# Output products of a threshold-attention and SwiGLU kernel: one level of seven-product blocks against two

## The chip, the cores and the metric

The kernel runs on one NeuronCore of a Trainium2 chip. Its five engines are TensorE (PE in the profile: matrix products into PSUM; PEld is its weight load), VectorE (DVE), ScalarE (ACT), GpSimd (POOL) and SyncE (SP, which here issues most of the DMAs). The metric is device time in microseconds, the median of several runs.

## The reference, cut to what matters

```
# q, k, v: (8, 8, 576, 64); w_gate, w_val: (512, 1536); w_out: (1536, 512), all float32
scores = matmul(q, k.T) / sqrt(64)
scores = where(scores >= max(scores) - tau, scores, -1e9)
attn   = exp(scores - max(scores));  attn = attn / (sum(attn) + 1e-9)
x      = matmul(attn, v)             # heads joined: x is (4608, 512)
g      = x @ w_gate
out    = (g * sigmoid(g) * (x @ w_val)) @ w_out
```

## The kernel before, in words

**Chunks.** The 4608 tokens are worked in nine chunks of 512. Chunks 0 to 7 hold the first 512 tokens of each of the eight batch entries, chunk 8 the 64 remaining tokens of all of them. For each chunk there are three kinds of TensorE work: attention (scores, L1173, and attention times values, L1260), gate and value products (`Group`, products issued at L890) and output products (`Outputs`, L1054).

**Seven products for eight.** Gate and value work is done in the Strassen-Winograd manner: a 2x2 block product takes seven block products and some sums of blocks. For the output product the two token halves of a unit of 256 tokens, the two halves of the 1536 inner columns and the two halves of the 512 output columns are the 2x2 blocks. So each of a chunk's two units has seven products (`one` to `seven`), each six matmuls with 128 tokens held and 256 output columns moved. Sums of the gated values (`half_sums`, 128x256 each) are made on POOL (L768), or on DVE (L771) in the tail. The results are added up in SBUF by DVE (L1073), POOL and ACT, and stored.

**Gated values.** `Group.finish` makes them: tanh on ACT (L943), a product on DVE (L944), a product on POOL (DVE in the tail). A group is 256 of the 1536 columns; a chunk has six groups of seven products (`p1` to `p7`), four matmuls each. Four of the seven weight operands of a group stay in SBUF (`wgv`, with one difference written over a quarter of it); the other three are sums that were computed once, stored in HBM (`sums_hbm`) and are loaded for each group into one of the two halves of `ring`.

**Slots.** From chunk 0 on the work is interleaved. A slot (`kk`, 0 to 19 for each batch entry `b`) is one tile of queries of a pair of heads: 128 queries, or 64 in the last of each five. In a slot TensorE first does the scores (`slot_scores`, two PSUM tiles; they must have been read by the slot before), in every fifth slot (`kk` 1, 6, 11, 16) the attention product of the five slots before, and then a written-out number of products as filler: `GV[kk]` steps of gate and value products of chunk `b-1`, then `CH[kk]` output products. Meanwhile DVE finds the maxima (L1195), ACT takes exponentials (L1209), DVE masks and sums (L1210), ACT and POOL scale (L1240, L1237), DVE transposes (L1241). After the last slot of `b` = 7 comes the tail, without softmax: the last attention, then chunks 7 and 8 with gate, value and output products only. There POOL's sums go to DVE.

**Order.** A planner (`Plan`) orders the small work while the program is built: each `job` has an engine, an assumed duration, dependencies and a rank (0 first); `pe` places TensorE work in program order. On the chip each engine runs its list in order and waits on semaphores.

**Early part.** Chunk 0's attention is done before the slots, with some 128x128 products (L450, L452, which turn the attention weights) that occur nowhere else.

Of the kernel before, what the change touches and what calls it, by code (L numbers as in the profile page):

```python
# [108 lines left out]
def kernel(  # L109
# [11 lines left out]
    nc = tc.nc  # L121
# [52 lines left out]
    wgv = const.tile([P, 2, NCC, DFF], F32, name="wgv")  # L174
    wo = const.tile([P, 2, NF, DM2], F32, name="wo")
    extra = const.tile([P, 3 * WS], F32, name="extra")
    ring = const.tile([P, 2, 3 * HW], F32, name="ring")
# [4 lines left out]
    ob = const.tile([P, 2, DM], F32, name="ob")  # L182
    sums_hbm = hbm.tile([NF2, P, 3 * HW], F32, name="sums_hbm")
    last_hbm = hbm.tile([P, NCC, B * (S - SM)], F32, name="last_hbm")

    rall = ring.rearrange("p s n -> p (s n)")
# [46 lines left out]
    los = deque([extra[:, 4 * S + 2 * TW:], rall[:, 4 * S:], ob.rearrange("p i n -> p (i n)")[:, 0:TW]])  # L233
# [529 lines left out]

    def ring_part(s, n):
        return ring[:, s, n * HW:(n + 1) * HW].rearrange("p (k f) -> p k f", k=2)

# [47 lines left out]
    def weight_sums(g, place, *deps):  # L814
# [5 lines left out]
        stores[g] = job("SP", 0.1, lambda: nc.sync.dma_start(out=sums_hbm[g], in_=place), j, lag=4.0)  # L820
# [6 lines left out]
    loads = {}  # L827

    def load_sums(c, g, *deps):
        loads[c, g] = job("SP", 0.1, lambda: nc.sync.dma_start(out=ring[:, g % 2], in_=sums_hbm[g]), stores[g], *deps, lag=4.0)  # L830
# [47 lines left out]
    class Group:  # L878


        def __init__(self, c, g):
            self.c, self.g = c, g
            self.b = None

# [9 lines left out]
        def ring_w(self, n):  # L894
            return ring_part(self.g % 2, n)

# [5 lines left out]
        def p1(self, early=True):  # L902
            self.a = take("pa")
            self.m1 = self.mul(self.a, pair_cols(wval, 0, self.g), x_block(self.c, 0, 0), True, *self.a.deps, *ready_x[self.c][0])
            self.a.bank.full = True
            if early:
                self.take_b()

        def p5(self):
            self.take_b()  # L910
            self.e = take("pe")
            m = self.mul(self.e, self.ring_w(0), xs[0], True, loads[self.c, self.g], *ready_x[self.c][1], *self.e.deps)
# [5 lines left out]
        def p2(self):  # L918
# [5 lines left out]
            m = self.mul(self.a, pair_cols(wval, 1, self.g), x_block(self.c, 0, 1), False, self.cb if self.b else self.s1)  # L924
            self.m2 = m

        def p6(self):
            u = self.u1_buf
            if self.b:
                m = self.mul(self.b, self.ring_w(1), xs[1], False, self.cb, *ready_x[self.c][2])  # L930
            else:
                b = self.b = take("pb")
                m = self.mul(b, self.ring_w(1), xs[1], True, *ready_x[self.c][2], *b.deps)
# [3 lines left out]
            self.u1 = job("ACT", 0.55, lambda: nc.scalar.activation(u.ap, self.b.rows(), AF.Copy, scale=0.5), m, *self.u1_old, rank=0)  # L937

# [550 lines left out]
```

## Time and profile before

| | us |
|---|---|
| median of three runs | 1440.7 (1439.89 to 1440.7) |
| profiled execution, its own time | 1440.44 |
| its span | 1438.7 |
| early part, to the first interleaved slot | 0 to 143 |
| interleaved slots (`b` = 1 to 7) | 143 to 1200 |
| period of an interleaved chunk | 154.5 |
| chunk 7 in the tail | 1215.8 to 1325.3 |
| chunk 8 in the tail | 1325.3 to 1438.7 |
| last output product ends | 1434.2 |

The DMA engines moved 77 GB/s in the mean and up to 203 GB/s in one fortieth of the span (slice 2). In the lines of the profile, "xN" is a number of records and "mean" is for one record; the columns after the bar are the busy time in us, the mean duration in ns, and the time that the engine sat idle just before such instructions, with what ended it. An answer on stretches lists, for each, its length and for each engine the busy time in us and the number of instructions, then the clock granted to TensorE, the DMA share and GB/s. A timeline line has the start, the length from first start to last end, the engine, line, operation and the number of records; the durations of neighbouring matmul records overlap, so their spacing is read from the starts. A wait line has the total, the number of times and the longest.

### The profile page before, as it was taken

The page shows a single profiled execution, that of the slowest core. Times are in us where ns is not written, and L with a number is a line of the kernel's source. Part 1 is how long each engine was busy: PE and PEld are TensorE (multiplying, and loading weights), DVE is VectorE, ACT ScalarE, POOL GpSimd, SP SyncE. Part 2 cuts the span into 40 slices and gives each one's busy share as a digit, 9 for nine tenths or more (in the row PEclk, how much of TensorE's full clock was granted, in tenths as well). Part 3 has the DMA queues.
Part 4 walks back from the last instruction along what each step waited for, and adds up shares of the span by engine and source line. Part 5 has one row for each costly group of instructions (what it writes and reads, how often), then busy time and mean ns, then how long its engine had stood idle before and what let it go on. Part 6 is the DMA issues. An engine that isn't in the chain of part 4 may idle for free.

```text
span 1438.7 us, 31145 instructions
## 1 busy us (share of the span) xinstructions
PE 1400.7 (97%) x11496; PEld 1078.7 (75%) x11496; DVE 1061.6 (74%) x3045; ACT 794.0 (55%) x2170; POOL 697.8 (49%) x686
## 2 busy tenths in 40 slices
PE   9999899999999999999999999999999999999998
PEld 6676666777777777777777777777777777888887
DVE  7988999888777878788788877887788874343343
ACT  6888765566646665566546664566556652220220
POOL 2465759965574448444754466445745462000000
PEclk9999999999999999999999999999999999999999
DMA  8734312353223312333232222332223311112101
GB/s 177 203 120 133 66 34 79 115 139 78 56 71 87 79 49 63 82 78 78 56 81 54 72 78 50 95 78 54 63 69 78 78 39 56 66 45 80 64 25 30
DMA packets 192071, 111.47 MB, mean 77 GB/s; under 512 B 165040, under 2 KB 166064, under 8 KB 191920
## 3 DMA queue, kind: packets, MB, share of 16 engines
q1 hardware_dynamic: 188320, 109.05, 28.5%
q8 instruction: 92, 1.51, 0.5%
q10 hardware_dynamic: 3600, 0.43, 0.2%
q14 instruction: 59, 0.48, 0.1%
HBM read 94.24 MB, written 15.20 MB: 76 GB/s over the span
## 4 chain that ended last, share of the span: by engine, by line
PE 76%; DVE 13%; ACT 6%; issue 2%; SPq 2%; DMA 1%; DVEq 0%; ACTq 0%
PE po L1054 22%; PE pb L890 14%; PE pa L890 10%; PE pe L890 10%; PE xa L1260 8%; PE sc L1173 7%; DVE pall L1210 3%; DVE mx L1195 2%; ACT pall L1209 2%; DVE pall L1241 1%; DVE mx L1201 1%; SPq L317 1%; DVE hall L944 1%; PE pv L498 1%; ACT sums L1224 1%
## 5 line engine op out<-in xcount | busy, mean ns | idle before, releaser
L1237 POOL TENSOR_SCALAR pall<-pall,ri 128x288 f32<-128x288 f32 x224 | 223.7, 1012 | 154.5 <-DVE ri L1230 153.4
L1210 DVE SCALAR_TENSOR_TENSOR pall<-sc,th,pall 128x288 f32<-128x288 f32 x504 | 233.1, 510 | 64.4 <-ACT pall L1209 63.3
L1209 ACT ACTIVATE pall<-sc,nm 128x288 f32<-128x288 f32 x504 | 213.6, 495 | 9.0 <-DVE pall L1210 9.0
L1195 DVE TENSOR_REDUCE mx<-sc 128x2 f32<-128x576 f32 x252 | 179.3, 747 | 38.2 <-PE sc L1173 37.2
L1054 PE MATMUL po<-wo,hall 128*128 128x256 f32 x852 | 196.2, 382 | 1.3 <-DVE hall L944 0.9
L1054 PEld LDWEIGHTS po<-wo,hall 128*128 128x128 f32 x852 | 159.6, 190 | 34.5 <-issue 5.8
L890 PE MATMUL pb<-xall,ring 128*128 128x256 f32 x768 | 184.5, 383 | 0.0
L890 PE MATMUL pa<-xall,wgv 128*128 128x256 f32 x768 | 183.3, 381 | 0.0
L1241 DVE STREAM_TRANSPOSE pall<-pall 128x1152 f32<-128x1152 f32 (+1 forms) x140 | 174.9, 1251 | 6.0 <-ACT pall L1240 3.5
L1205 ACT ACTIVATE th<-nm,cut 128x4 f32<-128x4 f32 (+1 forms) x140 | 41.5, 297 | 243.7 <-DVE nm L1202 219.6
L890 PEld LDWEIGHTS pb<-xall,ring 128*128 128x128 f32 x768 | 143.4, 190 | 31.9 <-issue 10.8
L1173 PE MATMUL sc<-kT,qT 64*32 64x288 f32 x4032 | 156.6, 410 | 9.1 <-DVE pall L1210 7.6
L890 PEld LDWEIGHTS pa<-xall,wgv 128*128 128x128 f32 x768 | 144.1, 190 | 27.6 <-ACT tmp L916 2.8
L768 POOL TENSOR_TENSOR hall<-hall,tmp 128x512 f32<-128x512 f32 x79 | 100.5, 1275 | 104.8 <-DVE hall L944 58.1
L1224 ACT COPY sums<-sums 32x4 f32<-32x4 f32 (+1 forms) x560 | 108.4, 194 | 74.7 <-DVE pall L1210 66.0
L1240 ACT ACTIVATE pall<-pall,ri 128x288 f32<-128x288 f32 x280 | 133.9, 529 | 26.6 <-DVE ri L1230 25.2
L1260 PE MATMUL xa<-pall,vall 64*64 64x288 f32 x2016 | 135.7, 409 | 12.3 <-DVE pall L1241 8.7
L1260 PEld LDWEIGHTS xa<-pall,vall 64*64 64x64 f32 x2016 | 88.4, 134 | 58.7 <-DVE pall L1241 12.0
L1173 PEld LDWEIGHTS sc<-kT,qT 64*32 64x32 f32 x4032 | 59.0, 105 | 79.2 <-issue 49.1
L1054 PE MATMUL po<-extra,ring 128*128 128x256 f32 x432 | 97.8, 382 | 0.6 <-DVE ob L1073 0.6
L1054 PEld LDWEIGHTS po<-extra,ring 128*128 128x128 f32 x432 | 80.9, 190 | 17.5 <-POOL hall L768 3.3
L890 PE MATMUL pe<-xall,ring 128*128 128x256 f32 x384 | 92.0, 382 | 0.0
(171 smaller groups left out, 2152.1 us busy)
## 6 DMA issues: line engine op xcount, KB each, us to landing
ring<-sums_hbm SPq DMA_DIRECT2D x48, 768.0 KB, 4.5
vall<-in_v_dram SPq DMA_DIRECT2D x112, 144.0 KB, 2.9
out_dram<-ob SPq DMA_DIRECT2D x32, 256.0 KB, 2.1
qT<-in_q_dram SPq DMA_DIRECT2D x112, 72.0 KB, 3.4
kT<-in_k_dram SPq DMA_DIRECT2D x112, 72.0 KB, 2.8
wo<-in_moe_w_gate_dram SPq DMA_DIRECT2D x16, 384.0 KB, 3.6
wo<-in_moe_w_val_dram SPq DMA_DIRECT2D x16, 384.0 KB, 4.1
sums_hbm<-ring SPq DMA_DIRECT2D x4, 768.0 KB, 4.2
```

Of the source, the lines that this page charges most:

```text
L768: return lambda: nc.gpsimd.tensor_tensor(out=out, in0=a, in1=b, op=op)
L890: nc.tensor.matmul(ps[:, i], w[:, k_, i * P:(i + 1) * P], x[:, k_, :], start=first and i == k_ == 0, stop=True, skip_group_check=True)
L1054: nc.tensor.matmul(ps, h(f), w[:, f, :], start=(f == 0), stop=(f == NF2 - 1))
L1173: nc.tensor.matmul(ps[g * G:(g + 1) * G, h, 0:SH], qT[hs, col:col + G], kT[hs, c * SH:(c + 1) * SH], start=True, stop=True)
L1195: rs.append(job("DVE", 0.72, lambda x=x, tile_=tile_: nc.vector.tensor_reduce(out=mx[:, 2 * x:2 * x + 2, 0], in_=tile_[:, :, 0:SH], axis=A ...
L1209: ej = job("ACT", 0.42, lambda x=x: nc.scalar.activation(ps[x], scs[x], AF.Exp, bias=nm[:, x:x + 1]), ej, rank=0)
L1210: mj = job("DVE", 0.45, lambda x=x: nc.vector.scalar_tensor_tensor(out=ps[x], in0=scs[x], scalar=th[:, x:x + 1], in1=ps[x], op0=ALU.is_ge, ...
L1224: nc.scalar.copy(sm[g * G:(g + 1) * G, 0:m, 1], sm[o * G:(o + 1) * G, 0:m, 0])
L1237: scaled.append(job("POOL", 1.02, lambda x=x: nc.gpsimd.tensor_scalar(out=ps[x], in0=ps[x], scalar1=ri[:, x:x + 1], scalar2=None, op0=ALU. ...
L1240: scaled.append(job("ACT", 0.46, lambda x=x: nc.scalar.activation(ps[x], ps[x], AF.Copy, scale=ri[:, x:x + 1]), rj, rank=2))
L1241: seg["turned"].append(job("DVE", 0.72 * len(pss), lambda: nc.vector.transpose(out=whole, in_=whole), *scaled, rank=2 if t < NT else 1))
L1260: nc.tensor.matmul(holds[a].ap()[h * D:(h + 1) * D, 0:SH].rearrange("d (i q) -> d i q", q=G), vr[rs, h, j, :], p[rs, h, :, j, :], start=(j ...
```

## The change

For chunks 2 to 8 the output product of a whole chunk (512 tokens) is done by a class `Deep` instead of `Outputs`. Its outer 2x2 blocks are 256 tokens, 768 inner columns and 256 output columns; each of the seven outer products is itself split into seven products of blocks of 128 tokens, 384 inner columns and 128 output columns (`product`, 49 in all, three matmuls each with 128 moved columns). An outer product's seven inner results stand side by side in two PSUM banks (896 columns). The outer additions are made by letting a product accumulate onto the banks of an earlier one after ACT has copied the earlier state to SBUF (`copies`), or by DVE adds; the inner ones are made once per output block in `combine`, four small additions. The sums of gated values are made in two layers: 128x512 outer sums (`sum`) and four 128x384 sums for each outer operand (`inner_sums`), shared between DVE and POOL.

The seven outer weight operands are split further once, by `deepen` (28 sums on POOL, in slots 2 to 8 of `b` = 3); the results lie where `wgv` was. So from chunk 2 on all seven weight operands of a gate and value group are loaded from HBM for each group, in two parts (`load_flow`), into `flow`, which covers the old `ring` and part of `wgv`; `store_plain` writes the four plain ones there once. `Deep` also uses `flow` for its sums and asks for the next chunk's loads when it is done with them.

The slots are laid out anew: other numbers in `GV` (for chunk 1 too), `CD` for the deep output steps, and in the nine slots of `BY_ACT` ACT does all four scalings instead of POOL two. In the tail `Deep` has an order of its own.

```diff
+    whole = const.tile([P, OB + 2 * NCC * DFF + 2 * 3 * HW], F32, name="big")
+    obs, big = whole[:, 0:OB], whole[:, OB:]
+    wgv = big[:, 0:2 * NCC * DFF].rearrange("p (m c f) -> p m c f", m=2, c=NCC)
-    ring = const.tile([P, 2, 3 * HW], F32, name="ring")
+    ring = big[:, 2 * NCC * DFF:].rearrange("p (s n) -> p s n", s=2)
+    flow = big[:, 2 * NCC * DFF + 2 * 3 * HW - 2 * GW:]
+    deeper = big[:, 0:NQ * 3 * QW]
...
+    def store_plain(g, *deps):
+
+        js = []
+        for n, w in ((0, pair_cols(wval, 0, g)), (1, pair_cols(wval, 1, g)), (5, pair_cols(wgat, 1, g)), (6, pair_cols(wgat, 0, g))):
+            js.append(job("SP", 0.1, lambda n=n, w=w: nc.sync.dma_start(
+                out=sums_hbm[g][:, n * HW:(n + 1) * HW].rearrange("p (k f) -> p k f", k=2), in_=w), *deps, lag=4.0))
+        plain_stores[g] = js
...
+    def load_flow(c, g, part, *deps):
+        lo, to = ((0, 4), (4, NQ))[part]
+        s = g % 2 * GW
+        loads[c, g, part] = job("SP", 0.1, lambda: nc.sync.dma_start(
+            out=flow[:, s + lo * HW:s + to * HW], in_=sums_hbm[g][:, lo * HW:to * HW]), stores[g], *plain_stores[g], *deps, lag=6.0)
...
+            ways = (lambda: pair_cols(wval, 0, g), lambda: pair_cols(wval, 1, g), lambda: ring_part(g % 2, 0), lambda: ring_part(g % 2, 1),
+                    lambda: ring_part(g % 2, 2), lambda: pair_cols(wgat, 1, g), lambda: pair_cols(wgat, 0, g))
+            self.w = [way() if c < DEEP else flow_part(g % 2, n) for n, way in enumerate(ways)]
+            self.w_deps = [[loads[c, g] if n in (2, 3, 4) else parts[g] if n == 6 else None] if c < DEEP else
+                           [loads[c, g, n // 4]] for n in range(NQ)]
...
+            if self.c >= DEEP and self.g + 2 < NF2:
+                load_flow(self.c, self.g + 2, 0, plan.t + plan.PIPE)
...
             if self.g + 2 < NF2:
-                load_sums(self.c, self.g + 2, m)
+                if self.c < DEEP:
+                    load_sums(self.c, self.g + 2, m)
+                else:
+                    load_flow(self.c, self.g + 2, 1, m)
...
+    operands = w11, w21, w22, ws4, w12, ws2, ws3
...
+    def quarters(a):
+
+        h = NF2 // 2
+        return [a[:, y * h:(y + 1) * h, x * P:(x + 1) * P] for y in range(2) for x in range(2)]
+
+    def deepen(o, *deps):
+        b11, b12, b21, b22 = quarters(operands[o])
+        t1, t2, t4 = (deeper_part(o, n) for n in range(3))
+        j = job("POOL", 1.0, pool_tt(t1, b12, b11, ALU.subtract), *deps, rank=3)
+        j = job("POOL", 1.0, pool_tt(t2, b22, t1, ALU.subtract), j, rank=3)
+        j = job("POOL", 1.0, pool_tt(t4, b21, t2, ALU.subtract), j, rank=3)
+        deep_jobs[o] = [job("POOL", 1.0, pool_tt(b12, b22, b12, ALU.subtract), j, rank=3)]
...
+            KW = NF2 * TC
+            self.s2, self.s3 = (flow[:, lo:lo + KW].rearrange("p (f n) -> p f n", n=TC) for lo in (GW, GW - KW))
+            self.early_place, self.late_place = flow[:, 0:KW], flow[:, 2 * GW - KW:2 * GW]
...
+            if tail[0]:
+                self.steps = deque([self.p1, self.gates_end, self.p2, self.p7_alone, self.p5, self.p6_alone, self.p3, self.p4_alone])
+                self.spaces = [pall[:, n * CW:(n + 1) * CW] for n in range(5)]
+            else:
+                self.steps = deque([self.p1, self.gates_end, self.p2, self.p5, self.p6, self.p3, self.p7, self.p4])
+                self.spaces = [*spaces, None, spaces[1]]
+            self.ready["a11"] = [gated[c, 0, x] for x in range(NF2 // 2)]
+            self.inner_sums(0, self.a11, self.early_place, self.ready["a11"], mark)
...
+        def early(self, mark):
+            c, n = self.c, NF2 // 2
+            j3 = [self.sum(self.s3, self.a11, self.a21, ALU.subtract, x, self.ready["a11"][x], gated[c, 1, x], mark) for x in range(n)]
+            self.ready["s3"] = j3
+            self.ready["s1"] = [self.sum(self.a21, self.a21, self.a22, ALU.add, x, j3[x], gated[c, 1, n + x]) for x in range(n - 1)]
+            if tail[0]:
+                self.inner_sums(6, self.s3, pall[:, 5 * CW:5 * CW + NF2 * TC], j3)
+
+        def late(self, mark):
+            c, n = self.c, NF2 // 2
+            self.ready["a12"] = [gated[c, 0, n + x] for x in range(n)]
+            self.ready["a22"] = [gated[c, 1, n + x] for x in range(n)]
+            j3 = self.ready["s3"]
+            self.inner_sums(1, self.a12, self.a11, self.ready["a12"], self.m1, *j3)
+            self.ready["s1"].append(self.sum(self.a21, self.a21, self.a22, ALU.add, n - 1, j3[n - 1], gated[c, 1, NF2 - 1], dve=True))
+            self.inner_sums(4, self.a21, self.late_place, self.ready["s1"], mark)
+            self.ready["s2"] = [self.sum(self.s2, self.a22, self.s3, ALU.subtract, x, j3[x], gated[c, 1, n + x], mark, rank=1) for x in range(n)]
+            self.inner_sums(5, self.s2, self.early_place, self.ready["s2"], self.m1)
...
+        def inner_sums(self, o, a, place, ready, *deps):
+
+            a11, a21, a12, a22 = quarters(a)
+            flat = place if len(place.shape) == 2 else place.rearrange("p f n -> p (f n)")
+            s1, s2, s3, s4 = (flat[:, n * QW:(n + 1) * QW].rearrange("p (f q) -> p f q", q=P) for n in range(4))
+            tt, eng, took = (dve_tt, "DVE", 0.49) if tail[0] or o in self.BY_DVE else (pool_tt, "POOL", 1.0)
+            rank = 1 if o in (1, 4, 5) else 2
+            j3 = job(eng, took, tt(s3, a11, a21, ALU.subtract), *ready, *deps, rank=rank)
+            j1 = job(eng, took, tt(s1, a21, a22, ALU.add), *ready, *deps, j3, rank=rank)
+            j2 = job(eng, took, tt(s2, s1, a11, ALU.subtract), j1, rank=rank)
+            j4 = job(eng, took, tt(s4, a12, s2, ALU.subtract), j2, rank=rank)
+            self.inner[o] = [(a11, ready), (a12, ready), (s4, [j4]), (a22, ready), (s1, [j1]), (s2, [j2]), (s3, [j3])], [j1, j2, j3, j4]
+
+        BY_DVE = 1, 4, 6
+        BY_POOL = 2, 3, 6
+        ORDER = 0, 1, 3, 6, 4, 5, 2
+        AT = {0: (0, 0), 1: (0, 1), 5: (0, 2), 2: (0, 3), 3: (1, 0), 4: (1, 1), 6: (1, 2)}
+
+        def product(self, o, holds, first, *deps):
+            parts, _ = self.inner[o]
+            ws = weights_of(o)
...
+            for n in self.ORDER:
+                a, ready = parts[n]
+                bank_, at_ = self.AT[n]
+
+                def fn(n=n, a=a, bank_=bank_, at_=at_):
+                    ps = holds[bank_].ap()[:, at_ * P:(at_ + 1) * P]
+                    for f in range(NF2 // 2):
+                        nc.tensor.matmul(ps, a[:, f, :], ws[n][:, f, :], start=bank_ not in begun, stop=True, skip_group_check=True)
+                        begun.add(bank_)
+
+                m = pe(0.655, fn, *ready, *deps, *deep_jobs[o])
+            return m
...
+        def copies(self, out, holds, *deps, rank=0):
+
+            return [job("ACT", 0.57, lambda: nc.scalar.copy(out[:, 0:4 * P], holds[0].ap()), *deps, rank=rank),
+                    job("ACT", 0.46, lambda: nc.scalar.copy(out[:, 4 * P:CW], holds[1].ap()[:, 0:3 * P]), *deps, rank=rank)]
...
+            tt, eng, took, less = (pool_tt, "POOL", 0.75, 0.44) if not tail[0] and o in self.BY_POOL else (dve_tt, "DVE", 0.36, 0.23)
+            twice = lambda x: x.broadcast_to((P, 2, P))
+            j = job(eng, took, tt(y[:, x:x + 2], twice(q[:, 0:1]), q[:, 1:3], ALU.add), *deps, *ob_jobs[n], rank=1)
+            j = job(eng, took, tt(y[:, x + 3:free + 1:free - x - 3], twice(y[:, x + 1:x + 2]), q[:, 5:7], ALU.add), j, rank=1)
+            j = job(eng, less, tt(y[:, x + 1], y[:, x + 3], q[:, 3], ALU.add), j, rank=1)
+            j = job(eng, took, tt(y[:, x + 2:x + 4], twice(y[:, free:free + 1]), q[:, 4:6], ALU.add), j, rank=1)
+            return n, j
...
+        def p1(self):
+            self.x, deps = self.pair("px")
+            self.m1 = self.product(0, self.x, True, *deps)
+            self.c1 = self.copies(self.spaces[0], self.x, self.m1, *u_list[0].jobs, *u_list[1].jobs)
+
+        def p2(self):
+            m = self.product(1, self.x, False, *self.c1)
+            x, t, t1 = self.x, self.spaces[0], self.spaces[1]
+            c2 = self.copies(t1, x, m, *u_list[1].jobs, *u_list[2].jobs, *u_list[3].jobs)
+            n, self.j2 = self.combine(1, t1, *c2)
+            self.ship(0, 0, n, self.j2)
...
+                self.z = [job("ACT", 0.57, lambda: nc.scalar.copy(x[0].ap(), t[:, 0:4 * P]), c2[0], rank=0),
+                          job("ACT", 0.46, lambda: nc.scalar.copy(x[1].ap()[:, 0:3 * P], t[:, 4 * P:CW]), c2[1], rank=0)]
+            s4 = [self.sum(self.a12, self.a12, self.s2, ALU.subtract, x, m, self.ready["s2"][x]) for x in range(NF2 // 2)]
+            self.ready["s4"] = s4
+            self.inner_sums(3, self.a22, self.a11, self.ready["a22"], m)
+
+        def p5(self):
+            self.y, deps = self.pair("py")
...
+            self.c5 = self.copies(self.spaces[4], self.y, m, self.j2)
+            if 6 not in self.inner:
+                self.inner_sums(6, self.s3, self.a21, self.ready["s3"], m)
+            self.inner_sums(2, self.a12, self.late_place, self.ready["s4"], m)
+
+        def p6(self):
+            m = self.product(5, self.x, False, *self.z)
+            self.next_flow(0, 0, m)
+            self.next_flow(1, 0, m, *self.ready["s4"])
+            self.c6 = self.copies(self.spaces[2], self.x, m, *n_list[0].jobs, *n_list[1].jobs)
...
+        def p7(self):
+            m = self.product(6, self.x, False, *self.c6)
+            t0, t1 = self.spaces[0], self.spaces[1]
+            self.c7 = self.copies(t0, self.x, m, *self.z)
+            tt, eng, took = (dve_tt, "DVE", 1.05) if tail[0] else (pool_tt, "POOL", 2.25)
+            self.v = job(eng, took, tt(t0, t0, t1, ALU.add), *self.c7, *self.c5, rank=1)
+            n, j = self.combine(6, t0, self.v)
+            self.ship(1, 1, n, j)
...
+            self.next_flow(0, 1, m)
...
+        def p7_alone(self):
+            x, deps = self.pair("px")
+            self.m7 = self.product(6, x, True, *deps)
+            self.c7 = self.copies(self.spaces[3], x, self.m7)
...
+        def p6_alone(self):
+            x, deps = self.pair("px")
+            m = self.product(5, x, True, *deps)
+            t = self.spaces
+            self.c6 = self.add(t[2], x, t[0], m, *self.c1)
+            tt = lambda out, a, b, *deps: job("DVE", 1.05, dve_tt(out, a, b, ALU.add), *deps, rank=1)
+            self.u3 = tt(t[3], t[2], t[3], *self.c6, *self.c7)
+            n, j = self.combine(6, t[4], tt(t[4], t[3], t[4], self.u3, *self.c5))
+            self.ship(1, 1, n, j)
+            self.next_flow(0, 0, m)
+            self.next_flow(1, 0, m, *self.ready["s4"])
+            self.next_flow(0, 1, self.m7)
...
+        def p4_alone(self):
+            x, deps = self.pair("px")
+            m = self.product(3, x, True, *deps)
+            n, j = self.combine(3, self.spaces[1], *self.add(self.spaces[1], x, self.spaces[3], m, self.u3, self.j2))
...
+        def gates_end(self):
+            state["last_product"]()
+            self.late(plan.t + plan.PIPE)
+
+        def p3(self):
+            m = self.product(2, self.y, False, *self.c5)
+            t2 = self.spaces[2]
+            q = self.add(t2, self.y, t2, m, *self.c6)
+            n, j = self.combine(2, t2, *q)
+            self.ship(0, 1, n, j)
...
+        def p4(self):
+            m = self.product(3, self.x, False, *self.c7)
+            t1 = self.spaces[1]
+            c4 = self.copies(t1, self.x, m, self.v)
+            self.done(self.x, *c4)
+            n, j = self.combine(3, t1, *c4)
...
-            if x % 2 and t < NT:
+            if x % 2 and t < NT and not by_act:
...
             for fn in (new.p5, new.p2, new.p6, new.p3, new.p7):
                 fn()
+                if c >= DEEP and g == NF2 - 2 and fn == new.p6:
+                    state["deep"] = Deep(c, plan.t + plan.PIPE)
...
-    GV = {2: 4, 3: 3, 4: 3, 5: 4, 6: 1, 7: 4, 8: 3, 9: 3, 10: 3, 11: 2, 12: 4, 13: 4, 14: 3}
+    GV = {2: 3, 3: 3, 4: 3, 5: 5, 6: 2, 7: 3, 8: 2, 9: 4, 10: 3, 11: 2, 12: 3, 13: 3, 14: 5}
     CH = {16: 1, 17: 3, 18: 2, 19: 2, 0: 3, 1: 1}
+    BY_ACT = 1, 5, 6, 11, 12, 13, 15, 16, 18
+    CD = {15: 2, 16: 2, 17: 1, 18: 1, 19: 1, 0: 1}
     PLAIN = {5: 2, 6: 0, 10: 2, 11: 0}
     CH0 = {14: 1, 15: 3, 16: 0, 17: 2, 18: 2, 19: 2, 20: 3, 21: 1}
...
             gv_steps(GV[kk])
+            if c == DEEP and kk < 2 + NQ:
+                deepen(kk - 2, plan.t, *(j for js in plain_stores.values() for j in js), *summed)
             if kk == 14:
                 next(state["gv"], None)
...
+        if state["run"] and c - (kk < 2) >= DEEP:
+            out_steps(CD.get(kk, 0))
...
-            slot_rest(seg, t, pss, marks)
+            slot_rest(seg, t, pss, marks, b > DEEP and kk in BY_ACT)
...
+                store_plain(g, parts[g])
 
     tail[0] = True
-    out_steps(3)
+    out_steps(1)
     attend(halved[-1])
...
-        state["last_product"]()
+        begin_outputs(c)
+        out_steps(2)
```

## Prediction

> **What bounds the kernel now.** I first read the page's busy times with the stretches of one interleaved chunk (427.5 to 582.0) and of that chunk's outputs (543.5 to 599.5):
>
> ```profile
> PE 1400.7 (97%) x11496; PEld 1078.7 (75%) x11496; DVE 1061.6 (74%) x3045; ACT 794.0 (55%) x2170; POOL 697.8 (49%) x686
> core 0: us, PE busy (x) PEld busy (x) DVE busy (x) ACT busy (x) POOL busy (x), PEclk, DMA share, GB/s
> 427.50:582.00 154.50, 152.57 (x1369) 115.02 (x1368) 123.75 (x378) 92.13 (x270) 85.00 (x89) 1.00 0.28 70
> 543.50:599.50 56.00, 55.84 (x529) 41.25 (x528) 44.31 (x140) 28.52 (x90) 35.88 (x43) 1.00 0.27 74
> ```
>
> TensorE is busy 152.57 of 154.50 us at full clock. A busy PE proves little, so next come its waits in that chunk:
>
> ```profile
> PE xa L1260 <- DVE pall L1241: 1.5, 1, 1.5
> PE xa L1260 <- DVE hall L944: 0.3, 1, 0.3
> PE po L1054 <- DVE hall L944: 0.2, 1, 0.2
> ```
>
> Two microseconds in 154.5: the matmul stream itself sets the pace, and every TensorE microsecond removed can shorten the run if nothing else becomes late. VectorE is second (44.31 of 56.00 around the outputs, 79%).
>
> **Price of one matmul.** The timeline shows today's output products and, early in the kernel, the shape that the change brings (128x128 moved against 128x128 held); the last line gives that shape's minimum, median and maximum:
>
> ```profile
> 13.54 1.16 PE L452 MATMUL tp<-pall 128*128 128x128 f32 x8
> 1309.72 2.75 PE L1054 MATMUL po<-extra,hall 128*128 128x256 f32 x12
> 1312.32 2.75 PE L1054 MATMUL po<-wo,hall 128*128 128x256 f32 x12
> 1314.90 5.34 PE L1054 MATMUL po<-extra,ring 128*128 128x256 f32 x24
> L452 PE MATMUL tp<-pall x128: 275/275/377, 13.5 to 58.8; 128*128 128x128 f32 x128
> ```
>
> One fp32 matmul is two records: a product of six is x12. From 1312.32 to 1314.90 twelve records take 2.58 us, 0.216 each (durations overlap, so starts are subtracted). For 128 columns: 1.16 us less the last record's 0.275 leaves 0.885 for seven steps; the first record is 0.102 longer (377 against 275), an uncovered weight load, so a step is (0.885 - 0.102)/7 = 0.112.
>
> **TensorE per deep chunk.** Removed: 2 halves x 7 products x 12 records = 168 x 0.216 = 36.3 us. Added: 7 x 7 blocks x 6 records = 294 x 0.112 = 32.9. Saved 3.4 us, over seven chunks **24.0 us**. This is the whole possible gain; the rest is what it costs.
>
> The Trainium skill speaks against it: "TensorE: Matmul & The Clock Gate", Back-to-back issue gap, says that in a stream of weight loads and matmuls 128 columns take about 81 ns, where moving alone would take 56, since the load isn't hidden. Scaled to fp32's two passes that is an estimated 0.16 us a record, 47 us a chunk, some 76 us lost in seven. Row L452 has a weight load before each matmul too and keeps 0.112, so I go by the row.
>
> What L452 can't show: each block of three starts with a possible semaphore wait on its weight load. At 0.216 a step the waits in the products are free (1309.72, 1312.32 and 1314.90 are 2.60 and 2.58 apart), but a load then has twice the matmul time to hide in. Bounds per block: 0, and the uncovered 0.102. I take 0, the price of satisfied waits in the product rows, and keep 49 x 0.102 = 5.0 us a chunk for the range.
>
> **The other engines,** by these rows:
>
> ```profile
> L768 POOL TENSOR_TENSOR ring<-hall 128x256 f32<-128x256 f32 x84 | 61.1, 745 | 1.5
> L768 POOL TENSOR_TENSOR tmp<-tmp 128x512 f32<-128x512 f32 x36 | 45.9, 1274 | 57.9 <-ACT tmp L966 57.9
> L1237 POOL TENSOR_SCALAR pall<-pall,ri 128x288 f32<-128x288 f32 x224 | 223.7, 1012 | 154.5 <-DVE ri L1230 153.4
> L771 DVE TENSOR_TENSOR hall<-hall,tmp 128x512 f32<-128x512 f32 x24 | 16.6, 691 | 0.8
> L1073 DVE TENSOR_TENSOR ob<-ob,po 128x256 f32<-128x256 f32 x107 | 43.5, 413 | 51.9 <-PE po L1054 51.2
> L1240 ACT ACTIVATE pall<-pall,ri 128x288 f32<-128x288 f32 x280 | 133.9, 529 | 26.6 <-DVE ri L1230 25.2
> L900 ACT COPY pb<-pa 128x512 f32<-128x512 f32 x47 | 27.3, 580 | 40.2 <-PE pa L890 29.3 <-DVE hall L944 10.9
> ```
>
> Halfway between 256 and 512 columns, a 384-wide inner sum is 1.01 us on POOL, 0.55 on DVE; 384 more columns of a copy on ACT, some 0.47.
> - POOL per interleaved chunk: out 24 half sums x 0.74 and two output adds, 19.2 us, and 18 scalings in nine slots (18.2, moved to ACT). In: 11 outer sums (14.0), 16 inner sums (16.1), three combinations of 2.65 (8.0), one 896-wide add (2.1), 40.2 in all. Net +2.8: 85.0 becomes 88 of 151.
> - ACT: 18 scalings at 0.529 (9.5) and seven copies of 1.05 (7.4) in, four of 0.37 out: +15.4, 92 becomes 107 of 151. Off the path.
> - DVE: 12 adds (5.0) out; one outer sum, 12 inner sums, one combination (1.5) and one add of 1.24 in (10.1). In the output stretch 44.3 becomes 49.4 while that stretch shrinks to 52.6: **94%**. Here is the danger.
> - Preparing the seven weight operands: 28 POOL sums, 28 us once, while POOL has 66 idle in that chunk and the first is due only at slot 15: nothing; with that cover gone, 28.
> - Streaming: 1.75 MB instead of 0.75 per group and 6 MB of stores. In the tail a group takes 28 x 0.432 = 12.1 us, so 152 GB/s; slice 2 of the page shows 203. A part is asked for nine products (15.5 us) ahead; 768 KB land in 4.5. On SP's queue the loads wait for products 5 to 7 and for group ends, ahead of the next q, k and v loads, due slots later. Nothing; if late, each group waits.
>
> **Slots.** A slot's scores need the banks of the slot before, freed by the masks of L1210. Where TensorE had filler enough, the second mask ended 4.8 to 6.6 us after the slot's first score and the next score started 0.15 later. Before, full slots were 6.5 to 11 us long. Now slot 8 has two products, 1.33 + 3.45 = 4.8 us, and slots 17, 18, 0 and 1 have some 6.0. At best (5.36 needed) slot 8 waits 0.6, with a loaded DVE 1.5; the other four 0 to 0.9 each. I take 1.0 and 4 x 0.12: 1.5 per chunk, 7.5 in five, and 1.0 for chunk 1, which gets slot 8 too.
>
> **New waits.** TensorE runs in order: behind a product that waits stand the next slot's scores, and behind them the whole softmax. Each deep product but the first of a bank pair waits for two copies of the product before it in the same banks (1.05 us on ACT, before product 5 another 1.05 back); between them lies at least a slot's scores (1.3) or another product (4.7): 0, except at the hand-over below. The tightest is product 2 in slot 18. From the last gate on, POOL has 1.3 (gate), 3.8 + 4.0 (for product 5), 2.9 (token sums after the attention of slot 16), 3.8 (S4), 4.0 (for product 3), 4.0 (for product 2) and 2.0 (scalings of slot 17) to do, 25.8 us, from 1.5 us after the last gate product; product 2's last block is due after 1.3 + 4.5 + 2 x 4.7 + 1.3 + 4.7 + 1.3 + 4.0 = 26.5. That is 0.8 late, so 0 to 2 a chunk; the operand for product 3 isn't needed until slot 0 and can be passed over, so I take 0.
>
> **Hand-over and end.** At the hand-over to the tail three products stood before the last attention and one behind it; now one stands before it and none behind. The last product waits for two copies (1.3), the first gate product for the attention's copies (some 1.3); the 0.6 before 1200.68 goes: +2.0. After the last matmul an add of 0.42 becomes 1.24 plus a combination of 1.5: +2.3. In the tail DVE's work per output stretch grows from 17.1 to some 30 of 35 us, still under TensorE.
>
> **Sum** against the profiled run's 1440.44 (span 1438.7): -24.0 + 7.5 + 1.0 + 2.0 + 2.3 = -11.2, so 1429.2. The runs' median is 0.26 higher: **1429.5**.
>
> **Rivals.**
> - DVE becomes the bound of the output stretch. For: the 94%; in chunk 0's stretch (120 to 260) it was 125.6 of 140 and TensorE waited. Against: transposes can slide past the stretch. At that stretch's 90%, 49.4 needs 54.9 us: +2.3, with slot 8 3.3 instead of 1.5 per chunk: 1438.5.
> - Slower: the weight load at the start of each block stays uncovered, at all 49 blocks of a chunk. For: load (192 ns as shown) and matmul now leave no slack. Against: satisfied waits cost nothing today. 343 x 0.102 = 35: 1464.5. It decides from 11.2/343 = 0.033 us a block.
> - The saving isn't there: the step is longer than 0.112 in this use. At 0.117 (11.2/2058 more) nothing remains; at 0.124, +13: 1454.
>
> **Chances.** Forecast as reckoned, 0.62 (1413 to 1437; the low end drops all waits); DVE bound, 0.15, half of it within the noise; uncovered loads or a longer step, 0.23, a few of these partly offset. About 0.2% (2.9 us) is what a measurement can tell from no change. Faster 0.68, same 0.09, slower 0.23; range 1413 to 1456.
>
> **What would show it.** Right: some 2058 records of the new product line, steps of 0.112; chunks 2 to 6 with a period near 152.6 instead of 154.5; TensorE's waits for L1210 at slot 8 only, about 1 us; the tail's two chunks some 3 us shorter each, less the end. Wrong: steps of 0.21 at each block's start; TensorE waiting for inner sums on DVE or POOL in slots 16 to 18; waits for the weight stream in the tail.

## Result and the profile after

| | before | after |
|---|---|---|
| median of four runs, us | 1440.3 (1438.74 to 1440.7) | 1513.55 (1507.39 to 1515.85) |
| ratio, 95% interval | | 1.0504 [1.0472, 1.0536] |
| span of the profiled execution | 1438.7 | 1511.5 |
| period of an interleaved deep chunk | 154.5 | 170.7 to 173.5 |
| from the last slot's scores to the end | 244.7 | 233.8 |

The change costs 73 us where 11 were forecast as gained. From the last slot's scores to the end it is 10.9 us shorter, 6.1 of which is output work that now stands ahead of these scores (84 records of 0.112 are left behind them, where there were 72 of 0.216); the loss sits in the interleaved chunks. The page's busy line and chain of after:

```profile
PE 1410.4 (93%) x12378; PEld 1114.6 (74%) x12378; DVE 1168.1 (77%) x3135; ACT 862.8 (57%) x2318; POOL 756.0 (50%) x691
PE 57%; DVE 22%; SPq 7%; ACT 6%; DMA 4%; issue 3%; POOL 1%; DVEq 0%; ACTq 0%; POOLq 0%
```

TensorE was to lose 24 us of busy time and has gained 10; SyncE's queue and a DMA are on the chain that ended last. The next view lists stretches: one deep chunk, and two pieces inside it (the first column is the stretch, then its length; PEclk is the granted clock).

```profile
core 0: us, PE busy (x) PEld busy (x) DVE busy (x) ACT busy (x) POOL busy (x), PEclk, DMA share, GB/s
600.50:771.30 170.80, 156.53 (x1499) 120.41 (x1498) 137.21 (x385) 104.77 (x296) 91.51 (x84) 0.96 0.37 101
672.00:684.40 12.40, 10.47 (x102) 7.60 (x100) 8.26 (x23) 6.58 (x20) 3.30 (x4) 1.00 0.71 169
684.50:691.30 6.80, 5.34 (x46) 3.88 (x49) 5.43 (x17) 2.82 (x7) 4.33 (x4) 0.50 0.01 2
```

DVE's 137.2 is 8.3 more than the predicted 123.75 + 10.1 - 5.0 = 128.9; POOL's 91.5 and ACT's 104.8 are near the predicted 88 and 107. And inside the chunk lies a piece of 6.8 us in which TensorE is granted half its clock. Who waited, first TensorE's waits, then one of DVE's (total, times, longest):

```profile
PE sc L1487 <- DVE pall L1524: 49.6, 27, 5.4
PE xa L1574 <- DVE hall L983: 23.8, 14, 3.8
PE py L1302 <- DVE big L789: 4.8, 8, 0.6
```

```profile
DVE kT L1616 <- DMA kT<-in_k_dram: 39.9, 14, 4.3
```

The direct wait for sums (4.8) is small. TensorE stands at the scores of a next slot and at the attention, as DVE is late; and DVE itself stands 39.9 us for keys (`kT`), a wait that before's list of DVE's waits does not have.

**The keys, followed once.** SyncE's queue, before and after, then TensorE of after, DVE of before and DVE of after at the same place (start, length, instructions):

```profile
651.98 0.34 SPq L830 DMA_DIRECT2D ring<-sums_hbm  x1
652.69 2.30 SPq L317 DMA_DIRECT2D qT<-in_q_dram  x4
655.03 4.43 SPq L317 DMA_DIRECT2D kT<-in_k_dram  x4
```

```profile
669.68 5.50 SPq L864 DMA_DIRECT2D big<-sums_hbm  x2
675.60 2.71 SPq L328 DMA_DIRECT2D qT<-in_q_dram  x4
678.35 3.67 SPq L328 DMA_DIRECT2D kT<-in_k_dram  x4
```

```profile
681.27 1.20 PE L1487 MATMUL sc<-kT,qT 64*32 64x288 f32 x32
685.96 7.26 PE L1574 MATMUL xa<-pall,vall 64*64 64x288 f32 x72 [3.49 <-DVE hall L983]
```

```profile
663.91 0.77 DVE L1302 STREAM_TRANSPOSE kT<-kT 128x576 f32<-128x576 f32 x1
```

```profile
684.55 0.78 DVE L1616 STREAM_TRANSPOSE kT<-kT 128x576 f32<-128x576 f32 x1 [3.69 <-DMA kT<-in_k_dram]
685.25 0.65 DVE L983 SCALAR_TENSOR_TENSOR hall<-vall,pa 128x512 f32<-128x512 f32 x1
```

Before, the eight loads of the next pair's queries and keys started 5.2 us ahead of slot 10 (657.90); the last had landed at 661.6, 2.4 us before DVE's transpose of the keys (663.91). After, they start 0.8 us behind its start (674.76), when a streamed weight load ahead of them in the list has had its product. DVE works in order: its transpose of the keys waits 3.69 us, and behind it stands a gate product (L983) that has long had its data and that frees the bank which the attention needs. TensorE idles 3.49 us (682.47 to 685.96), and 2.0 us into this wait, at 684.5, its granted clock falls to 0.50, where it stays for 6.8 us: the attention takes 7.26 us where it took 4.90 before (4.60 at other slots). Slot 11 lasts 15.5 us instead of 11.1. From `b` = 4 on DVE also waits for keys in slot 1 (1.2 to 3.0 us) and slot 5 (2.8 to 4.3); those of slot 16 are on time.

The Trainium skill, "TensorE: Matmul & The Clock Gate", Part 1 (What's actually happening), says that TensorE falls to half its clock after an idle window of about 3.4 us. This trace agrees in the half clock and differs in the time: the clock fell after 2.0 us of idling, and in the 3.4 us before its fall TensorE had still been busy for 1.4.

**The sums.** Groups of DVE's sums in after, by shape (busy total, then mean ns of one). The first five lines mix interleaved chunks and tail or stand in the chunks alone; the last two are the tail's part (from 1300):

```profile
L789 DVE TENSOR_TENSOR hall<-big 128x384 f32<-128x384 f32 x10 | 13.1, 1348 | 0.0
L789 DVE TENSOR_TENSOR big<-hall 128x384 f32<-128x384 f32 x22 | 20.0, 940 | 3.9 <-PE pa L930 3.9
L789 DVE TENSOR_TENSOR hall<-hall 128x384 f32<-128x384 f32 x36 | 23.5, 674 | 1.3
L789 DVE TENSOR_TENSOR big<-hall,big 128x384 f32<-128x384 f32 x11 | 10.3, 939 | 0.5
L789 DVE TENSOR_TENSOR big<-big,tmp 128x256 f32<-128x256 f32 x12 | 11.8, 984 | 0.9
```

```profile
L789 DVE TENSOR_TENSOR big<-hall 128x384 f32<-128x384 f32 x12 | 6.3, 552 | 3.9 <-PE pa L930 3.9
L789 DVE TENSOR_TENSOR big<-big,pall 128x256 f32<-128x256 f32 x16 | 6.8, 423 | 0.4
```

In the tail a 384-wide sum takes 0.55 and a 256-wide one 0.42, just as priced. In the chunks the ten `big<-hall` sums take (20.0 - 6.3)/10 = 1.37, `hall<-big` 1.35 and the combinations' 256-wide sums 0.98. POOL is at its own sums meanwhile (in the stretch from 736.6 to 753 its timeline has no gap). Set side by side by their starts and ends, twenty of the sixty inner sums that DVE has in the chunks overlap no sum of POOL, and each of these takes 0.55 to 0.56; the forty others take 1.31 in the mean (four of them 0.55).

### The profile page after: what moved, and what is told of

Read it like the earlier page. It is cut to its first block, busy times and chain, and to the rows that moved or that the text cites. A ratio compares the mean times of both kernels' runs of the same rounds, so it can differ in the third digit from the quotient of the medians.

```text
span 1511.5 us, 33248 instructions
## 1 busy us (share of the span) xinstructions
PE 1410.4 (93%) x12378; PEld 1114.6 (74%) x12378; DVE 1168.1 (77%) x3135; ACT 862.8 (57%) x2318; POOL 756.0 (50%) x691
## 4 chain that ended last, share of the span: by engine, by line
PE 57%; DVE 22%; SPq 7%; ACT 6%; DMA 4%; issue 3%; POOL 1%; DVEq 0%; ACTq 0%; POOLq 0%
PE pb L930 12%; PE pe L930 9%; PE pa L930 8%; PE xa L1574 6%; SPq L328 6%; PE sc L1487 6%; PE po L1096 5%; PE py L1302 3%; DVE pall L1524 3%; PE px L1302 3%; DVE big L789 3%; DVE mx L1509 3%; DMA kT<-in_k_dram 3%; DVE pall L1555 2%; ACT pall L1523 2%
## 5 line engine op out<-in xcount | busy, mean ns | idle before, releaser
L930 PE MATMUL pb<-xall,big 128*128 128x256 f32 x1104 | 264.7, 382 | 0.0
L930 PEld LDWEIGHTS pb<-xall,big 128*128 128x128 f32 x1104 | 206.0, 190 | 43.0 <-issue 13.8
L1551 POOL TENSOR_SCALAR pall<-pall,ri 128x288 f32<-128x288 f32 x134 | 134.2, 1013 | 171.7 <-DVE ri L1544 171.1
L930 PE MATMUL pe<-xall,big 128*128 128x256 f32 x768 | 182.7, 381 | 0.0
L930 PE MATMUL pa<-xall,big 128*128 128x256 f32 x752 | 182.3, 385 | 0.0
L1519 ACT ACTIVATE th<-nm,cut 128x4 f32<-128x4 f32 (+1 forms) x140 | 41.3, 295 | 237.6 <-DVE nm L1516 201.8
L930 PEld LDWEIGHTS pa<-xall,big 128*128 128x128 f32 x752 | 141.5, 191 | 33.1 <-ACT tmp L953 7.9
L930 PEld LDWEIGHTS pe<-xall,big 128*128 128x128 f32 x768 | 144.9, 190 | 24.8 <-issue 2.8
L1515 DVE TENSOR_REDUCE mx<-mx 32x4 f32<-32x4 f32 (+1 forms) x560 | 83.1, 148 | 10.4
L786 POOL TENSOR_TENSOR tmp<-tmp 128x512 f32<-128x512 f32 (+1 forms) x41 | 56.2, 1372 | 69.0 <-ACT tmp L1005 54.5
L1614 POOL TENSOR_SCALAR qT<-qT,scl 128x576 f32<-128x576 f32 x27 | 47.3, 1751 | 69.3 <-DMA qT<-in_q_dram 35.2
```

Of the source, the lines that this page charges most:

```text
L786: return lambda: nc.gpsimd.tensor_tensor(out=out, in0=a, in1=b, op=op)
L930: nc.tensor.matmul(ps[:, i], w[:, k_, i * P:(i + 1) * P], x[:, k_, :], start=first and i == k_ == 0, stop=True, skip_group_check=True)
L1551: scaled.append(job("POOL", 1.02, lambda x=x: nc.gpsimd.tensor_scalar(out=ps[x], in0=ps[x], scalar1=ri[:, x:x + 1], scalar2=None, op0=ALU. ...
```

## Experiments

"Late keys" below is the first theory (weight loads stand ahead of the key loads on SyncE), "sums" the second (DVE's two-operand sums run slow beside POOL). The first three kernels ran together against 1440.8.

**1. Late keys alone.** The planner is told what the eight loads take in after, 5.8 us from the first issue to the last and some 3 to land, and so asks for them earlier (it also orders DVE's list anew):

```diff
-        fj = job("SP", 0.8, fetch, later_than, lag=3.5)
+        fj = job("SP", 5.8, fetch, later_than, lag=3.2)
```

> One number of the planner is changed: the eight q and k loads of a slot group are reckoned at 5.8 us of issue instead of 0.8, so DVE's transposes of the keys are placed later in its list; nothing else of the chip's work changes. Theory 'late keys' (the loads stand in SP's queue behind a weight load that waits for a product, and DVE's list runs into the keys before they land): DVE's wait for kT falls from 39.9 us to under 10, slot 11 from some 15.4 us to under 10.5, slots 1 and 6 by 1 to 3 us; 8 to 11 us for each of the five deep interleaved chunks, so 1458 to 1473 us instead of 1513. Theory 'shared port' alone (DVE's two-input sums are slow beside POOL's): slots 16 to 18 keep their 38.7 us, and without late keys being a cause the time stays within 5 us of 1513. Rival 'too much DVE work': DVE's list is as long as before, 1505 to 1520.

Measured: 1455.44, ratio 1.0112 [1.0089, 1.0134]: 58 us come back, 3 more than the range had. DVE's wait for keys:

```profile
DVE kT L1616 <- DMA kT<-in_k_dram: 3.8, 4, 1.3
```

Slot 11 is 9.31 and slot 1 5.66 in `b` = 5 (14.14 and 8.72 in after). Period 158.2, mean clock 0.989. Slots 16 to 18 shrink too, from 38.2 to 33.9 in `b` = 5, though no keys were late there, so not all of the 58 us is the keys' price. Slots 3 and 4 grow from 12.6 to 15.6, mainly by a new wait (gate and value products for L983, 6.9 in all).

**2. Sums alone.** In the interleaved part DVE's outer and inner sums become block transposes of their first operand, and the second operand is left out, with any wait for it. The combinations stay.

```diff
+    def dve_one(out, a, b, op):
+        return lambda: nc.vector.transpose(out=out, in_=a)
...
-            tt, eng, took = (dve_tt, "DVE", 0.49) if tail[0] or o in self.BY_DVE else (pool_tt, "POOL", 1.0)
+            tt, eng, took = (dve_tt if tail[0] else dve_one, "DVE", 0.49) if tail[0] or o in self.BY_DVE else (pool_tt, "POOL", 1.0)
```

> In the interleaved part the DVE's outer and inner sums of the gated values are replaced by block transposes of their first operand: as many DVE instructions of the same size, but with one SBUF input instead of two; the second operand is left out of these sums. Theory 'shared port': each 128x384 takes some 0.53 to 0.6 us instead of 0.9 to 1.6, slots 16 to 18 fall from 38.7 to some 29, TensorE's waits for L1524 fall by more than half; 1460 to 1475 us instead of 1513. Rival 'too much DVE work': number and size are unchanged, so 1500 to 1515. Theory 'late keys' alone: no change, slot 11 stays at 15 us in every case.

Measured: 1470.54, 1.0216 [1.0194, 1.0237]: 43 us come back. Slots 16 to 18 of `b` = 5 are 28.8 instead of 38.2 long; slot 11 stays at 14.4, and the keys stay late:

```profile
DVE kT L1619 <- DMA kT<-in_k_dram: 43.1, 14, 5.2
```

**3. Both.**

> Both edits of a_lag and b_one_input together (the second operand of DVE's interleaved sums is left out). If the two causes are all of it, the period of a deep interleaved chunk returns from 171 to 151 to 154 us and the time to 1410 to 1430; each cause alone leaves 1460 to 1475. Rival 'too much DVE work': above 1450 still, with slots 17 to 1 limited by L1524.

Measured: 1433.92, 0.996 [0.9945, 0.9975], period 154.8, clock 0.998. That is 79.6 us below after, while 58 and 43 make 101: the two edits share some 21 us (both shorten slots 16 to 18). The time lies 4 us above the expected range. What waits is left (TensorE):

```profile
PE sc L1490 <- DVE pall L1527: 21.0, 26, 1.3
PE pe L933 <- DVE hall L986: 6.8, 4, 1.7
PE py L1305 <- POOL big L786: 3.9, 4, 1.0
```

It is a yardstick and no candidate, since it leaves operands out: with both edits all but 4.4 us of the distance between 1513.55 and the predicted 1429.5 is gone. That it comes so near is in part luck: the period of 154.8 is 2.2 above the predicted 152.6 and no shorter than before's 154.5, and the tail makes up for some of it (see the hand-over below).

**4. The port by itself.** A small kernel, 24 instructions of 128x384 in each stage: DVE's sum of two SBUF operands alone, beside POOL sums, beside POOL scalings (one operand); a DVE transpose beside POOL sums; a DVE sum with one PSUM operand beside POOL sums; DVE sums beside ACT copies.

```diff
+    for _ in range(N):
+        nc.vector.tensor_tensor(out=dc[:, 0:W], in0=da[:, 0:W], in1=db[:, 0:W], op=ALU.subtract)
+        nc.gpsimd.tensor_tensor(out=pc[:, 0:W], in0=pa[:, 0:W], in1=pb[:, 0:W], op=ALU.subtract)
```

> The disputed cost alone: 24 DVE additions of 128x384, two SBUF inputs, first alone, then beside POOL additions of two inputs, beside POOL scalings of one input, then DVE block transposes beside POOL additions, DVE additions with one PSUM input beside POOL additions, and DVE additions beside ACT copies. Nothing of the reference is computed. Theory 'shared port': 0.55 us alone and beside ACT; 1.0 to 1.6 beside POOL additions; beside POOL scalings something between; transposes and the PSUM form 0.55 to 0.6 beside POOL. Rival: 0.55 in all stretches, and the long sums in the kernel come from something else (PSUM, DMA writes).

Measured, in the page's groups; L59 is alone, L65 and L66 ran together, then L69 with L70, L73 with L74, L77 with L78; L62 is POOL alone, L81 beside ACT:

```profile
L70 POOL TENSOR_SCALAR pc<-pa 128x384 f32<-128x384 f32 x24 | 29.4, 1226 | 2.0
L65 DVE TENSOR_TENSOR dc<-da,db 128x384 f32<-128x384 f32 x24 | 29.6, 1233 | 0.8
L66 POOL TENSOR_TENSOR pc<-pa,pb 128x384 f32<-128x384 f32 x24 | 28.3, 1180 | 1.9
...
L62 POOL TENSOR_TENSOR pc<-pa,pb 128x384 f32<-128x384 f32 x24 | 23.8, 991 | 1.9
...
L69 DVE TENSOR_TENSOR dc<-da,db 128x384 f32<-128x384 f32 x24 | 15.6, 650 | 0.8
L73 DVE STREAM_TRANSPOSE dc<-da 128x384 f32<-128x384 f32 x24 | 13.9, 579 | 0.8
L59 DVE TENSOR_TENSOR dc<-da,db 128x384 f32<-128x384 f32 x24 | 13.4, 559 | 0.8
L77 DVE TENSOR_TENSOR dc<-sp,db 128x384 f32<-128x384 f32 x24 | 13.4, 557 | 0.9
```

559 ns become 1233 beside POOL sums, and POOL's own 991 become 1180. With one SBUF operand less DVE loses next to nothing: from PSUM 557, and a transpose takes 579 (in kernel 3 its mean is 0.55 us with a POOL sum beside it and without). The Trainium skill, "GPSIMD Engine Reference", section 1 (Specifications), row SBUF interfaces, states that POOL shares its interfaces with DVE and that DVE instructions with two SBUF inputs contend; these rows agree and give the price.

**5. Key loads early, nothing else.** Only SyncE's list is changed: the loads are issued right after the scores of the last slot that reads the old keys; the other lists stay.

```diff
-            box["t"] = load_qk(i)
+            box["t"] = early_qk.pop(i) if i in early_qk else load_qk(i)
...
+            if x == len(seg["tiles"]) - 1 and n + 2 < len(halved):
+                early_qk[i + 2] = load_qk(i + 2)
```

> Only the place of the q and k loads in SP's list is changed against the changed kernel: they are issued right behind the scores that free their buffer, five slots ahead of their old place's neighbour (ahead of the weight loads of the last slot of a group of five), while DVE's, POOL's and TensorE's lists and all weight traffic stay as they are. Theory 'late keys by SP's order': DVE's wait for kT falls from 39.9 us to under 5, slot 11 from 15 to 9.3, slot 1 from 8 to under 6; 1450 to 1462 us, as with a_lag (1455). Rival 'late keys by traffic' (the DMA engines are busy with 1 MB weight loads whatever the order): kT still waited for, over 25 us, and 1495 us or more.

Measured: 1469.01, 1.0201 [1.0183, 1.0219], against 1440.59 (so too in 6 to 8): 44.5 us come back, 7 less than the range asked. DVE's waits have no keys left, slots 11 and 6 are 9.31, the period is 160.4. So the keys were late by SyncE's order and not by the traffic of the streamed weights, which is unchanged here. Slots 16 and 17 stay at 18.37 and 11.47, so that what kernel 1 won there came from the planner's other order. In a non-deep chunk TensorE now waits 3.2 us behind an output store that the loads delay.

**6. No sums on DVE.** Kernel 5, with the interleaved inner sums and combinations on POOL and all scalings on ACT:

```diff
-        BY_DVE = 1, 4, 6
-        BY_POOL = 2, 3, 6
+        BY_DVE = ()
+        BY_POOL = 1, 2, 3, 6
...
-    BY_ACT = 1, 5, 6, 11, 12, 13, 15, 16, 18
+    BY_ACT = range(20)
```

> e_early, and the interleaved sums of the deep chunks all on POOL (none on DVE but the one for the last gate), with ACT doing all four scalings in every full slot. Theory 'shared port': without two-input sums on DVE slots 16 to 18 fall below 31 us in sum (38.7 in the changed kernel, 28.8 in b_one_input); if POOL can carry 16 us more a chunk, the chunk's period is 152 to 155 and the time 1425 to 1440. Rival 'POOL becomes the bound': TensorE waits for L786 in slots 16 to 19 and 0, 2 to 4 us a chunk, 1440 to 1455. Rival 'too much DVE work' can't tell here, since DVE's work shrinks too.

Measured: 1492.14, 1.0363 [1.0344, 1.0382], worse than kernel 5 and far above both expected ranges. POOL is the new bound at the deep products:

```profile
PE py L1302 <- POOL big L786: 33.0, 23, 1.9
```

**7. Deep from chunk 6 on, loads early.** Kernel 5's edit, with `DEEP = 6`, and the old `GV` and weight loads for the chunks before.

> e_early with the two-level products for chunks 6, 7 and 8 only (weights streamed, new slot layout and ACT's scalings from chunk 6 on; chunks 1 to 5 keep the old layout and the old products). The tail showed 233.8 us from the scores of its last slot to the end against 244.7 before, POOL standing still there. If the loss is only in the interleaved chunks, the periods of chunks 1 to 5 return to 154.5 and the time is 1440.8 - 10.9 + some 4 for chunk 6: 1431 to 1437. If streaming or the new layout of SBUF costs by itself, also in the tail: 1440 or more.

Measured: 1460.37, 1.0164 [1.012, 1.0208]. The miss has its reason in the early loads: in chunks that keep the old output products a store now stands behind them on SyncE,

```profile
584.52 2.59 SPq L328 DMA_DIRECT2D kT<-in_k_dram  x4
587.21 0.57 SPq L548 DMA_DIRECT2D out_dram<-big  x1
```

```profile
589.74 0.37 ACT L1109 COPY big<-po 128x256 f32<-128x256 f32 x1 [4.06 <-DMA out_dram<-big]
```

```profile
591.85 5.42 PE L1096 MATMUL po<-extra,big 128*128 128x256 f32 x24 [2.90 <-DVE big L1115]
```

ACT waits 4.06 us for the stored buffer, DVE behind it for ACT, TensorE for DVE, and slot 0 lasts 12.0 us instead of 9.1 (`b` = 4). The fix of one queue order was a new fault in another; kernel 9 has the same chunks deep without the early loads, and there these chunks keep their period.

**8. True prices for the planner.** Kernel 5, with DVE's interleaved sums told as 1.2 and 0.9 instead of 0.49 and 0.36 (the first of the two lines is shown).

```diff
-(dve_tt, "DVE", 0.49) if tail[0] or o in self.BY_DVE
+(dve_tt, "DVE", 0.49 if tail[0] else 1.2) if tail[0] or o in self.BY_DVE
```

> e_early with the planner told the durations that DVE's sums had beside POOL (1.2 us for 128x384 and 0.9 for the small additions instead of 0.49 and 0.36), so that it orders the lists by them; the work is the same. Theory 'shared port': the port stays contended, so the sums still take 0.9 to 1.5 us; the softmax is delayed less by a better order: 1440 to 1455, against 1450 to 1462 for e_early. Rival 'it is only the order': 1425 to 1435.

Measured: 1466.97, 1.0187 [1.017, 1.0204]: above the expected range, and with kernel 5's 1.0201 [1.0183, 1.0219] not told apart. Another order only moves the wait (TensorE for sums 17.6 instead of 4.8, for masks 18.8 instead of 41.3).

**9 and 10. Deep products where nothing collides.** Kernel 9: `DEEP = 6` with kernel 1's edit in place of kernel 5's. Kernel 10: `DEEP = 7`, key loads as in before, so that only the tail's chunks 7 and 8 are deep:

```diff
-    DEEP = 2
+    DEEP = 7
...
+    for o in range(NQ):
+        deepen(o, plan.t, *(j for js in plain_stores.values() for j in js), *summed)
     for c in (B - 1, B):
```

> Deep products only for chunks 6, 7 and 8 (one interleaved, two in the tail), gate and value weights streamed for 7 and 8 only, and the honest price for the q and k loads (5.8 us of issuing) instead of the early issue. If the losses of the change are the late keys and the sums beside POOL, the old chunks run at 154.5 as in the kernel before, chunk 6 costs 3.7 more (a_lag's 158.2), the tail gives back about 10.9 (233.8 against 244.7, from the last scores to the end, in which the longer end is already counted): about 1433 to 1437. If the layout or the streaming have a cost of their own in every chunk: above 1445.

> Deep products only for chunks 7 and 8, whose work lies behind the last slot, so that the four scalings, the inner sums and the streamed loads stand beside no slot at all; the 28 subtractions on POOL run beside the gates of chunk 7. Late keys and contention in slots: both gone, period 154.5. What is left is 7.6 to 8.2 saved (105.4 against 109.4 in chunk 7, the same in 8), 2.5 lost at the end: about 1435. If the subtractions on POOL slow DVE's gates (whose second operand comes from PSUM, which in the small kernel lost nothing beside POOL: 557 against 559 ns) or the first deep product waits for them: 1440 or more.

Measured in five rounds against 1439.09: kernel 9 1437.79, 0.9995 [0.9986, 1.0004], no difference, where 1433 to 1437 was expected; kernel 10 **1436.51, 0.9978 [0.997, 0.9987]**, faster than both kernels. Kernel 10's tail, where chunks 7 and 8 start:

```profile
1215.51 1.89 PE L930 MATMUL pa<-xall,big 128*128 128x256 f32 x8
1320.85 1.89 PE L930 MATMUL pa<-xall,big 128*128 128x256 f32 x8
```

Chunk 7 takes 105.3 instead of 109.4, chunk 8's products 105.5 instead of 108.9, and 7.1 us follow the last product instead of 4.5: 4.1 + 3.4 - 2.6, with 0.3 from an earlier start 5.2, which is the difference of the spans (1438.66 to 1433.43). The medians differ by 2.6. Kernel 9's chunk 6 costs more than it saves: `b` = 7 starts 0.2 us later than before, chunk 7 1.9 us later (1217.70 instead of 1215.84).

## Why the prediction was wrong, step by step

- **Price of a matmul, and uncovered loads at block starts: right.** The end of after's last deep product:

```profile
1500.82 0.83 PE L1302 MATMUL px<-big,hall 128*128 128x128 f32 x6
1501.49 0.83 PE L1302 MATMUL px<-extra,hall 128*128 128x128 f32 x6
1502.16 1.50 PE L1302 MATMUL px<-big,hall 128*128 128x128 f32 x12
1503.50 0.83 PE L1302 MATMUL px<-extra,hall 128*128 128x128 f32 x6
```

  Six records take 0.67, or 0.112 each, also where a block begins. The rivals of an uncovered load and of a longer step fall, and so does the estimate of 0.16 from the skill's gap. Chunk 7 in the tail is shorter by 4.0 (105.46); the end is 2.7 longer where 2.3 was forecast.
- **DVE's sums: the term that was mis-sized.** The 0.55 was taken halfway between two rows: L771, from the tail, where POOL does nothing, and L1073, which has one operand in PSUM. Where they run, the sixty inner sums of five chunks take 62.4 us, 1.04 each: (1.04 - 0.55) x 12 = 5.9 a chunk; a combination takes 3.7 instead of 1.5 (two sums of 0.98, one of 0.82 and one of 0.91), the outer sum 0.3 more: 8.4, which is the 8.3 of the stretch. By the prediction's own reckoning the output stretch then needs 49.4 + 8.4 = 57.8 us of DVE in 52.6: the "danger" was past 100%. Kernel 2 gives 43 us for most of these sums. The rival that came nearest (DVE bound, 1438.5) had the place and not the size.
- **Streaming: "Nothing; if late, each group waits" failed, and at another place.** The bandwidth was enough and no group waits for its weights; what is late is what stands behind the loads on SyncE. The sentence named the queue and the loads, and took "due slots later" unread: before's queue begins them 5.2 us ahead of slot 10, and the last lands 2.4 us before DVE takes the keys up; after's begins them 6.0 us later against the slot, which leaves 3.7 us to wait. Kernels 1 and 5 show it.
- **The clock: not in the sum at all.** Every wait was priced at its length. A wait of 3.5 us cost itself and a stretch at half clock that outlasted it by 5.3 us; the mean clock is 0.96 in the deep chunks, up to 7 us of 171.
- **Slots: too low.** Without the two causes (kernel 3) TensorE waits 21.0 for masks against 7.6 before, 13.4 more where 8.5 were forecast. The period is 154.8 against the predicted 152.6, which has the 1.5 of waits in it: even then a deep interleaved chunk takes as long as an old one. For `b` = 4 to 6 the 1.0 forecast at the end of slot 8 came in each chunk; further waits of 0.9 and 0.7 for masks (at the scores of slots 3 and 18), 1.7 for a gate product in slot 4 and 1.0 for a sum of POOL's were not in the forecast and use up the saving.
- **Hand-over: 2.0 forecast, none measured.** In after chunk 7 starts 15.7 us behind the last slot's scores instead of 21.9, and 6.1 of these 6.2 are the output work that has moved ahead; the waits on both sides are 0.7 and 0.6.
- **Product 2 in slot 18, POOL's load: nearly right.** POOL is at 91.5 where 88 was forecast. Product 2 was reckoned 0.8 late and put at 0; in kernel 3 it waits 1.0 for POOL's sums in four chunks (3.9 in all).

What stays open: why kernel 1 relieved slots 16 to 18 by 4 to 6 us a chunk while kernel 5, with the keys as early, won at most 1 there. The planner's order of DVE's list differs; which step of it counts was not tried alone.

## What to carry to other kernels

Price a VectorE sum of two SBUF operands from a row in which GpSimd is at sums of its own, if it will be at such sums; with an operand from PSUM, or in a part where GpSimd is idle, the plain price holds. When loads are added to a queue that works in order, list what stands behind each of them with the slack that it has today, issue time included; the victim is rarely the load itself. And a saving per matmul is best taken first where nothing else is near its bound: here two chunks out of seven held all of the gain.

## What was not expected of the hardware

- A DVE sum of two SBUF operands takes 2.2 times as long beside POOL sums (559 to 1233 ns), and POOL loses 19% (991 to 1180). Beside POOL scalings with one operand DVE loses 16% (650), while such a scaling takes 1226 ns for 384 columns, longer than a sum of two operands alone (991).
- In a wait of 3.49 us TensorE's clock fell to half, 2.0 us after the last matmul, and stayed there for 6.8 us; an attention product took 7.26 instead of 4.60 to 4.90, which adds two thirds or more to the wait's price.
- Eight loads of 72 KB occupy SyncE's queue for 4.6 to 8.4 us in after (median 6.4), 4.6 to 7.4 in before (5.7) and mostly 4.6 in kernel 5, longer than the last of them takes to land (3.0 us where the keys were followed in after).
